# Attention and MLP on one core: the probabilities of ScalarE and VectorE in one array of 40 blocks, and a new order of the work

## The chip, the cores and the metric

The kernel runs on one core of a Trainium2 chip. The metric is the device time of one execution in microseconds; the time before is the median of three runs. Besides the times there is a profile of one execution: the instructions of each engine with start and duration, and for each idle stretch the work that ended it. Engines are TensorE (PE, with its weight loads as PEld), VectorE (DVE), ScalarE (ACT), GpSimd (POOL) and SyncE (SP), which only issues DMAs.

## The reference

A multi-head attention block and a mixer with an MLP run on the same input, and a gate mixes them for each token. S = 2048 tokens, D = 512, 32 heads of 16, F = 1792; inputs and output are bf16.

```python
g = sigmoid((x * gate_w).sum(-1, keepdims=True))
a = attention(x, wqkv, wo)                      # softmax over all 2048 keys, 32 heads
h = gelu(layernorm(x) @ w1)                     # its four quarters are shifted by 1, -1, 2, -2 tokens: hs
x1 = x + hs @ w2
b = x1 + gelu(layernorm(x1) @ w3) @ w4
return g * a + (1 - g) * b
```

Nearly all of the time goes to the softmax: 32 x 2048 x 2048 = 134 million exponentials.

## The kernel before

**Tiles and rounds.** The attention is cut into 32 rounds. A round is a chunk of 512 queries, a group of 8 heads and the even or odd heads of that group, so four heads run at once, one in each quarter of TensorE's rows. In a round each of the four heads has 16 key tiles of 128 keys; that makes 64 score tiles of 128 keys x 512 queries in a round and 2048 in all. A score tile is one matmul (line 1293) with 32 rows of weights; four of them, one for each quarter, can run side by side. Its result fills one of the eight PSUM banks.

**Two ways to the exponential.** ScalarE takes two or three score tiles (two or three banks) in one ACTIVATE with Exp and writes bf16 probabilities into two or three blocks of `pa_all`, an array of 16 blocks of 512 (`issue_act`, line 1376; the instruction is line 1388). VectorE takes single tiles and computes the bits of the bf16 result directly: one multiply and add from PSUM to 16-bit integers (line 1418). That gives a piecewise linear exponential, so three more copies of it are made, with 32, 64 and 96 added to the bits (`close_pair`, line 1433); the weighted sum of the four is close to the exponential. Two tiles of VectorE make a pair, and the copies are made for the pair, 1024 wide. The first copy is always VectorE's (line 1456). Of the second and third, GpSimd makes the third, or both, or none (line 1458 is GpSimd's): `GP2` is the share of pairs for which it makes both, `1 - GP3` the share, besides the pairs near the end of a round (`URG`), that VectorE makes alone. The pair and its copies lie in four of 12 buffers `PD` of 1024 each. At most three pairs are under way, which the class `token` counts.

**Products.** A tile of ScalarE costs one product with V (line 1510, `take_pv`), a tile of VectorE four, one for each copy, the last two with V scaled by 0.707. Products and all projections run in column mode, four side by side, one in each quarter of the columns; the scores run in row mode. Products sum up in one accumulator bank for each round. Lines 975 (`gen`) are the projections of attention and MLP, which are put between the attention's work and evacuated mostly by VectorE. At the end of a round the sums are copied out (line 1530), the denominators go through DRAM to be spread, and GpSimd multiplies (line 1546).

**The order.** No engine chooses anything on the chip: the order of every engine's instructions is fixed at build time by a planner in the kernel, the class `Sim` (line 152), which plays the engines through in time with a hold and a latency for each job. An exponential holds ScalarE for `0.833 * 512 * w + 67` ns, the first step of VectorE's tile `533 * w + 65` ns, a copy of a pair 338 ns on VectorE or 1018 ns on GpSimd. Copies on VectorE and all GpSimd jobs are marked `port`: the planner lets only one of them run at a time (`lock`, line 293). In the program itself each GpSimd job waits for the VectorE copy that stands before it in that order (`in_port_order`, line 267).

`pe_pick` (line 1678) chooses what TensorE does next. First come score tiles for ScalarE: twice in a row it tries to prepare three or two tiles, if the banks held for exponentials stay within `CAP3` or `CAP2`. With them, or when VectorE runs dry (`DVE_ALONE`), come score tiles for VectorE, as long as fewer than `DVE_WAIT` wait and fewer than `LIMD` other banks are taken (`room`). Then it fills the time until the running exponential ends with projections and products; products come first when many are ready (`PRESS`) or when few blocks of `PA` or buffers of `PD` are free (`PA_LOW`, `PD_LOW`). Every 8 score tiles the constants of these rules are changed by the table `STEPS` (line 453), which has 233 entries with 1482 values. So the number of tiles that VectorE gets, the size of each visit of TensorE to the scores, and the order of all queues follow from this table and from the holds.

**Buffers.** `Run` (line 49) takes several slots of a class at once. Banks must lie side by side. Two blocks of `PA` are simply the two lowest free ones; three must be evenly spaced.

```python
        pr = evs["pair"] = {"h": 0, "buf": Buf("PD", 8), "token": Buf("token", 1), "jobs": [], "pv": []}
```

A `PD` buffer is free again when the last of its copies and products has read it, for both tiles of the pair. The products of a pair, also those of the unshifted tiles, are queued only when the pair is closed, and wait for the first steps of both tiles.

Of the kernel before, what the change touches and what calls it, by code (L numbers as in the profile page):

```python
# [11 lines left out]
ALU = mybir.AluOpType  # L12
BF16 = mybir.dt.bfloat16
# [84 lines left out]
class Job:  # L98
    __slots__ = ("eng", "hold", "lat", "deps", "prio", "fn", "acq", "frees", "at", "done", "start", "seq", "ready", "name", "port", "watch", "deps_tiles")

    def __init__(self, eng, hold, lat, deps, fn, prio=5, acq=(), frees=(), at=0, name="", port=False):
# [7 lines left out]
        self.watch = []  # L109

# [41 lines left out]
class Sim:  # L152
# [4 lines left out]
    def __init__(self, slots):  # L157
# [13 lines left out]
        self.lock = 0.0  # L171
        self.pending = 0
# [109 lines left out]
    def try_engine(self, e):  # L282
# [27 lines left out]
        if j.port:  # L310
            self.lock = self.t + j.hold
        self.busy[e] += j.hold
# [3 lines left out]
        self.push(self.t + j.hold + j.lat, lambda: self.finish_job(j))  # L316
# [60 lines left out]
def kernel(  # L377
# [63 lines left out]
        PD_LOW=1,  # L441
        PA_LOW=0,
# [7 lines left out]
        ROT=2, DUE_SH=-14, AT_SH=0, HOLE=7, MAXG=1, CAP2=4, CAP3=0, LIMD=3, RES=0, ACC2=0, LIMA=3, JOIN=0,  # L450
# [3 lines left out]
        0: dict(DVE_STOP=8, SL0=165, AHEAD2=16, PV_IDLE=0.117, MAXU=4, LIMD=4, LIMA=2),  # L454
        1: dict(DVE_STOP=6, DVE_WAIT=1, AHEAD=16, PV_IDLE=0.5, MAXU=3, AT_SH=69, LIMD=3, LIMA=3),
        2: dict(P1_PRIO=0.743, GP2=0.5, DVE_STOP_L=16, DVE_WAIT=3, AHEAD=3, PV_IDLE=0.731, PRESS=15, DUE_SH=16, CAP2=6,
            RES=1, JOIN=1),
        3: dict(P1_PRIO=0.414, S_PRIO=0.3, DVE_STOP=13, DVE_STOP_L=14, EARLY=64, AHEAD=9, AHEAD2=24, PV_FULL=0.947,
            PRESS=18, CAP2=5, CAP3=6, RES=0),
        5: dict(S_PRIO=0.38, DVE_STOP=8, DVE_ALONE=-158, EARLY=99, AHEAD=3, PV_FULL=0.813, MAXU=9, ROT=1, AT_SH=96,  # L460
            HOLE=2),
        6: dict(MAXU=2),
        7: dict(GP2=0.315, URG_L=18, DVE_ALONE=2, AHEAD=9, PRESS=26, MAXU=3, CAP3=5),
        8: dict(URG_L=12, AHEAD=12, PV_FULL=0.916, PRESS=18, MAXU=4, AT_SH=69, HOLE=7, ACC2=1),
        9: dict(P1_PRIO=0.743, S_PRIO=0.625, EARLY=64, AHEAD=9, AHEAD2=13, PV_FULL=0.947, PV_IDLE=0.117, MAXU=5, ROT=3,
            HOLE=2, CAP3=6),
        10: dict(AHEAD=12, AHEAD2=24, LIMD=2),
        11: dict(URG_L=18),
        12: dict(P1_PRIO=0.279, GP2=0.655, URG_L=12, EARLY=99, AHEAD=9, AHEAD2=13, PV_FULL=0.916, MAXU=3, ROT=0, HOLE=3,
            LIMD=3, ACC2=0),  # L470
        13: dict(P1_PRIO=0.55, GP2=0.315, EARLY=64, IDLE_NS=700, DVE_WAIT=4, AHEAD2=5, MAXU=4, HOLE=7, MAXG=2),
        14: dict(P1_PRIO=0.743, URG_L=18, IDLE_NS=537, DVE_WAIT=3, AHEAD=12, AHEAD2=24, PV_FULL=0.947, MAXU=5, ROT=3,
            HOLE=2, MAXG=1, LIMD=2, ACC2=1),
        15: dict(DVE_WAIT=2),
        16: dict(URG_L=12, DVE_WAIT=3, AHEAD=9, HOLE=0, LIMD=3),
        17: dict(P1_PRIO=0.279, GP3=1, HOLE=2, MAXG=2),
        18: dict(P1_PRIO=0.743, GP3=0.967, EARLY=99, SL0=45, IDLE_NS=374, PD_LOW=3, AHEAD2=5, PV_FULL=0.916, HOLE=7,
            MAXG=1, CAP3=0, ACC2=0),
        19: dict(DVE_ALONE=-158, EARLY=64, SL1=0, IDLE_NS=459, AHEAD2=24, PV_IDLE=0.5, ROT=0),
        20: dict(URG=8, URG_L=18, SL1=60, IDLE_NS=374, PD_LOW=1, PV_FULL=0.97, PV_IDLE=0.117, HOLE=2),  # L480
        21: dict(URG=5, URG_L=12, SL1=0, IDLE_NS=459, PD_LOW=3, PV_FULL=0.916, PV_IDLE=0.5, HOLE=7),
        22: dict(HOLE=3),
        23: dict(DVE_STOP_L=12, HOLE=7),
        25: dict(DVE_STOP_L=14, URG=8, DVE_ALONE=2, IDLE_NS=864, PD_LOW=1, PA_LOW=3, AHEAD2=13, ROT=3, AT_SH=96, CAP2=6,
            LIMD=4, JOIN=0),
        26: dict(DVE_STOP=4, URG=5, URG_L=18, SL1=60, IDLE_NS=700, PD_LOW=3, PA_LOW=0, DVE_WAIT=4, AHEAD2=24,
            PV_IDLE=0.117, AT_SH=69, CAP2=5, LIMD=3, JOIN=1),
        27: dict(GP3=1, DVE_STOP=8, URG=8, EARLY=99, SL0=100, SL1=0, PD_LOW=2, DVE_WAIT=3, AHEAD=7, PV_FULL=0.947,
            PV_IDLE=0.5, HOLE=2, LIMA=2),
        28: dict(URG_L=12, SL0=45, IDLE_NS=374, AHEAD=9, DUE_SH=-6, HOLE=7, LIMA=3),  # L490
        29: dict(P1_PRIO=0.136, GP3=0.967, EARLY=64, IDLE_NS=864, AHEAD2=13, PV_FULL=0.916, PV_IDLE=0.731, DUE_SH=16,
            AT_SH=96, CAP2=6, LIMD=4, JOIN=0),
        30: dict(P1_PRIO=0.743, S_PRIO=0.178, GP2=1, DVE_STOP_L=16, URG=11, IDLE_NS=374, AHEAD2=24, PV_IDLE=0.5, ROT=0,
            AT_SH=69, CAP2=4, ACC2=1, JOIN=1),
        31: dict(S_PRIO=0.625, DVE_STOP_L=14, EARLY=99, PV_IDLE=0.731, ROT=3, CAP2=5, ACC2=0, JOIN=0),
        32: dict(DVE_STOP_L=16, EARLY=64, IDLE_NS=459, PA_LOW=1, PV_FULL=0.947, PV_IDLE=0.5, ROT=0, LIMA=4),
        33: dict(S_PRIO=0.178, DVE_STOP_L=7, URG=3, IDLE_NS=374, PA_LOW=0, AHEAD=12, PV_FULL=0.916, PRESS=11, ROT=2,
            AT_SH=118, ACC2=1, LIMA=3, JOIN=1),
        34: dict(S_PRIO=0.625, DVE_STOP_L=14, URG=11, IDLE_NS=864, PD_LOW=3, AHEAD=9, AHEAD2=9, PV_IDLE=0.117, PRESS=18,
            ROT=0, AT_SH=69, ACC2=0, JOIN=0),  # L500
        35: dict(SL1=60),
        36: dict(P1_PRIO=0.414, SL1=0, ACC2=1),
        37: dict(P1_PRIO=0.743, ACC2=0),
        38: dict(DVE_STOP_L=16, DVE_ALONE=-158, IDLE_NS=459, PD_LOW=2, PA_LOW=1, AHEAD2=24, PV_FULL=0.947, PRESS=57,
            MAXU=3, CAP3=5, LIMA=4),
        39: dict(P1_PRIO=0.55, S_PRIO=0.214, DVE_STOP_L=14, URG=2, DVE_ALONE=2, SL0=0, PD_LOW=3, AHEAD=5, PV_FULL=0.916,
            PRESS=18, MAXU=2, CAP2=4, CAP3=0, ACC2=1, LIMA=2, JOIN=1),
        40: dict(P1_PRIO=0.743, S_PRIO=0.625, URG=11, DVE_ALONE=-81, SL0=45, PD_LOW=2, AHEAD=9, PV_IDLE=0.5, PRESS=11,
            MAXU=5, ROT=1, ACC2=0, LIMA=4, JOIN=0),
        41: dict(SL0=165),  # L510
        42: dict(S_PRIO=0.214, GP3=0.8, SL0=45, AHEAD=7, PV_IDLE=0.117, PRESS=43, MAXU=4),
        43: dict(DVE_STOP_L=7, HOLE=3, CAP3=6),
        44: dict(SL1=60),
        45: dict(S_PRIO=0.178, DVE_STOP=6, DVE_STOP_L=12, DVE_ALONE=2, SL0=0, SL1=0, IDLE_NS=864, PV_FULL=0.947,
            PRESS=26, HOLE=2, CAP3=0, JOIN=1),
        46: dict(IDLE_NS=537, MAXG=2),
        49: dict(IDLE_NS=459, DUE_SH=32, MAXG=1),
        50: dict(JOIN=0),
        51: dict(S_PRIO=0.3, IDLE_NS=537, JOIN=1),
        52: dict(S_PRIO=0.178, IDLE_NS=459, MAXU=5, DUE_SH=16),  # L520
        53: dict(IDLE_NS=864, MAXU=4),
        54: dict(IDLE_NS=459, DUE_SH=32, LIMA=2),
        55: dict(PD_LOW=3, LIMA=4),
        56: dict(DVE_ALONE=138, PD_LOW=2, PA_LOW=0, JOIN=0),
        57: dict(DVE_STOP=4, DVE_STOP_L=14, URG=8, DVE_ALONE=362, EARLY=99, PD_LOW=3, PA_LOW=1, PV_FULL=0.97, DUE_SH=16,
            MAXG=2, ACC2=1),
        59: dict(DVE_STOP=6, DVE_STOP_L=12, URG=11, DVE_ALONE=2, EARLY=64, PD_LOW=2, PV_FULL=0.947, MAXU=5, MAXG=1,
            ACC2=0, JOIN=1),
        60: dict(DVE_STOP=4, DVE_STOP_L=14, URG=8, DVE_ALONE=362, EARLY=99, PD_LOW=3, PV_FULL=0.97, MAXU=4, ROT=2,
# [1389 lines left out]
```

## Time and profile before

| | |
|---|---|
| median of 3 runs (lowest to highest) | 762.45 us (760.06 to 764.45) |
| the profiled execution, its own time | 761.38 us |
| its span, first to last instruction | 759.4 us |
| TensorE clock granted, mean | 0.999 of full speed |
| ScalarE: first exponential starts, last one starts | 10.3 us, 749.5 us |
| ScalarE's busy time besides exponentials | five Gelu instructions (31.8 us) and table loads (12.8 us) |
| GpSimd's idle time before line 1458 | 255.0 us |
| all 16 DMA engines, mean | 46 GB/s; 17.40 MB read and 6.81 MB written in HBM |

A row of the costliest groups gives the line, the engine and the operation, what it writes and reads with shapes, how often it ran, then the busy time in us and the mean duration of one in ns, then the engine's idle time just before such instructions and whose work ended it. Instructions of one engine overlap at their ends, so busy time divided by count is less than the mean duration. A matmul's end is modelled: a TensorE that is 98% busy isn't at its peak. A row of the waits gives engine and line, who was waited for, the total in us, how often and the longest.

### The profile page before, as it was taken

What the parts mean: (1) busy time and instruction counts of PE and PEld (TensorE: products, weight loads), DVE (VectorE), ACT (ScalarE), POOL (GpSimd) and SP (SyncE); (2) the same over time, 40 slices, a digit from 0 to 9 for tenths busy, and PEclk for the clock granted to TensorE, in tenths of its full rate; (3) what the DMA queues carried; (4) which work ended last, traced back from release to release, by engine and by line L of the source; (5) the groups of instructions that cost most, each with busy time, mean ns of one, the idle gap of its engine ahead of it and who ended that gap; (6) DMA issues with size and microseconds to landing.
All of it is one profiled execution on the core that took longest, in us unless ns stands there. A gap on an engine that the chain in (4) does not pass through costs nothing.

```text
span 759.4 us, 23495 instructions
## 1 busy us (share of the span) xinstructions
PE 746.4 (98%) x9545; PEld 218.2 (29%) x9545; DVE 704.9 (93%) x1428; ACT 735.6 (97%) x744; POOL 460.4 (61%) x458
## 2 busy tenths in 40 slices
PE   9999999999999999999999999999999999999997
PEld 5343222222322222223222222422223222222332
DVE  6999899999999999999998999898999999999966
ACT  6999999999999999999998999999999999999995
POOL 2334476776785456775645767465466577767732
PEclk9999999999999999999999999999999999999999
DMA  9433211231001320042101000202000001000001
GB/s 189 150 87 58 53 47 33 48 100 65 21 6 48 79 68 13 15 133 65 38 15 33 27 20 21 47 11 58 23 27 19 15 17 28 26 27 21 20 16 34
DMA packets 67091, 34.57 MB, mean 46 GB/s; under 512 B 46748, under 2 KB 62380, under 8 KB 66984
## 3 DMA queue, kind: packets, MB, share of 16 engines
q1 hardware_dynamic: 66040, 32.56, 17.6%
q8 instruction: 74, 1.21, 0.7%
q10 hardware_dynamic: 944, 0.52, 0.2%
q14 instruction: 33, 0.27, 0.1%
HBM read 17.40 MB, written 6.81 MB: 32 GB/s over the span
## 4 chain that ended last, share of the span: by engine, by line
PE 72%; ACT 10%; DVE 9%; issue 3%; DMA 2%; POOL 2%; SPq 1%; POOLq 0%; DVEq 0%; ACTq 0%
PE banks L1510 25%; PE banks L1293 25%; PE banks L975 21%; ACT pa_all L1388 10%; DVE PD L1418 4%; DVE PD L1456 3%; POOL PD L1458 2%; DMA oD<-oT 1%; DMA pk<-den 1%; DMA xn_dram<-xn 1%; PE banks L954 0%; PE banks L1840 0%; SPq L1550 0%; POOL oT L1546 0%; PE banks L996 0%
## 5 line engine op out<-in xcount | busy, mean ns | idle before, releaser
L1388 ACT ACTIVATE pa_all<-banks 128x1024 bf16<-128x1024 f32 x719 | 685.7, 1137 | 9.8 <-PE banks L1293 7.9
L1458 POOL TENSOR_SCALAR PD<-PD 128x1024 uint16<-128x1024 uint16 x396 | 407.7, 1051 | 255.0 <-DVE PD L1456 117.8
L1418 DVE TENSOR_SCALAR PD<-banks 128x512 uint16<-128x512 f32 x554 | 366.3, 685 | 27.9 <-PE banks L1293 24.1
L1510 PE MATMUL banks<-PD,V 128*17 128x512 bf16 (+1 forms) x2240 | 300.2, 382 | 3.3 <-DVE PD L1456 1.5
L1293 PE MATMUL banks<-q,kT 32*128 32x512 bf16 x2048 | 288.8, 384 | 2.5 <-ACT pa_all L1388 1.3
L1510 PE MATMUL banks<-pa_all,V 128*17 128x512 bf16 (+1 forms) x1488 | 269.3, 381 | 0.0
L1456 DVE TENSOR_SCALAR PD<-PD 128x1024 uint16<-128x1024 uint16 x444 | 192.0, 476 | 1.4
L1293 PEld LDWEIGHTS <-kT 32*128 32x128 bf16 x2048 | 72.5, 91 | 313.9 <-ACT pa_all L1388 296.0
L1510 PEld LDWEIGHTS <-V 128*17 128x17 bf16 (+1 forms) x3728 | 72.5, 88 | 122.5 <-issue 104.3
L975 PE MATMUL banks<-xnT,w 128*32 128x512 bf16 x1152 | 95.6, 383 | 0.4 <-DVE PD L1418 0.2
L975 PE MATMUL banks<-w,hT 128*32 128x512 bf16 x704 | 59.6, 382 | 0.0
L975 PEld LDWEIGHTS <-w 128*32 128x32 bf16 x1920 | 43.6, 95 | 45.6 <-issue 27.4
L1546 POOL TENSOR_TENSOR oT<-accsb,bcs 128x512 bf16<-128x512 f32 x31 | 39.5, 1275 | 25.2 <-DVE PD L1456 16.0
L975 PE MATMUL banks<-w,hB 128*32 128x512 bf16 x448 | 43.0, 383 | 0.0
L975 PE MATMUL banks<-w,w 128*32 128x256 bf16 (+1 forms) x768 | 41.3, 311 | 0.0
L975 PE MATMUL banks<-wo,oD 128*32 128x512 bf16 x224 | 29.9, 383 | 1.2 <-DMA oD<-oT 1.1
L1530 DVE COPY accsb<-banks 128x512 f32<-128x512 f32 x31 | 21.1, 679 | 3.6 <-PE banks L1510 3.0
L975 PE MATMUL banks<-w,wq 128*32 128x512 bf16 x256 | 22.8, 383 | 0.3 <-ACT w L1006 0.3
L975 PEld LDWEIGHTS <-hT 128*32 128x32 bf16 x704 | 16.6, 95 | 18.9 <-issue 12.1
L1122 DVE BATCH_NORM_STATS2 st<-x_sb 128x6 f32<-128x512 bf16 x32 | 21.6, 683 | 0.1
L1212 DVE CAST hB<-banks 128x512 bf16<-128x512 f32 x28 | 18.9, 680 | 1.5 <-PE banks L975 1.4
L1212 DVE CAST hT<-banks 128x512 bf16<-128x512 f32 x28 | 18.8, 680 | 0.8 <-PE banks L975 0.7
(90 smaller groups left out, 253.9 us busy)
## 6 DMA issues: line engine op xcount, KB each, us to landing
bcs<-rr SPq DMA_DIRECT2D x124, 64.0 KB
xn_dram<-xn SPq DMA_DIRECT2D x32, 128.0 KB
w<-in_B_w_dram SPq DMA_DIRECT2D x5, 512.0 KB
oD<-oT SPq DMA_DIRECT2D x124, 16.0 KB
w<-in_B_w_dram SPq DMA_DIRECT2D x4, 448.0 KB
out_dram<-ot SPq DMA_DIRECT2D x14, 128.0 KB
x_sb<-in_A_x_dram SPq DMA_DIRECT2D x3, 512.0 KB
w<-in_A_wqkv_dram SPq DMA_DIRECT2D x2, 256.0 KB
```

The costliest lines, as they stand in the source:

```text
L975: units.append([Op("col", j, lambda j=j, lf=lf, rf=rf, n0=n0, n1=n1, st=st, sp=sp: nc.tensor.matmul(get()[32 * j:32 * j + 32, n0:n1], lhsT ...
L1122: a = dve(600, deps, lambda: nc.vector.bn_stats(out=sb.slot[:], in_=x_sb[:, t, :]), prio=6, at=at, acq=[sb])
L1212: pre.append(evac(g, PSUM_NS, lambda ps, m=m: nc.vector.tensor_copy(out=h2()[:, m, :], in_=ps[:])))
L1293: o = Op("row", i, lambda: nc.tensor.matmul(dst(), lhsT=kT[G][32 * i:32 * i + 32, kt * P:(kt + 1) * P], rhs=qbuf[G, c].slot[32 * i:32 * i ...
L1388: job = act(hold, ops, lambda: nc.scalar.activation(out=pa_all[:, pb.cut(), :], in_=unit()[:, rb.cut(), :], func=ACT.Exp, scale=0.25), acq ...
L1418: return nc.vector.tensor_scalar(out=pr["buf"].slot[:].rearrange("p (b c) -> p b c", c=512)[:, h0:h0 + w, :], in0=unit()[:, rb.cut(), :], ...
L1456: return nc.vector.tensor_scalar(out=d[k][:, 0:w], in0=d[0][:, 0:w], scalar1=float(SHIFT * k), scalar2=None, op0=ALU.add)
L1458: return nc.gpsimd.tensor_scalar(out=d[k][:, 0:w], in0=d[0 if both else 2][:, 0:w], scalar1=1.0, scalar2=float(SHIFT * (k if both else 1)) ...
L1510: return nc.tensor.matmul(one(accs[r])[32 * i:32 * i + n, :], lhsT=lhs(n), rhs=rhs(), start=st and not edge, stop=True, tile_position=(0, ...
L1530: e = dve(PSUM_NS, round_ops[r], lambda: nc.vector.tensor_copy(out=ab.slot[:], in_=one(accs[r])), acq=[ab], prio=0, frees=[accs[r], Call(a ...
L1546: n = gp(1250, d3, lambda: nc.gpsimd.tensor_tensor(out=ob.slot[:], in0=ab.slot[:], in1=bb.slot[:], op=ALU.mult), acq=[ob], frees=[ab, bb], ...
```

## The change

**One array.** `pa_all` (16 blocks) and the 12 `PD` buffers become `prob`, 40 blocks of 512 16-bit values; ScalarE writes into it as bf16, VectorE and GpSimd as integers. The number of tokens is 3 in both.

```diff
-    NPA, NPD, NW = 8, 12, 9
+    NPROB, NTOK, NW = 40, 3, 9
...
-    pa_all = const.tile([P, 2 * NPA, 512], BF16, name="pa_all")
+    prob = const.tile([P, NPROB, 512], U16, name="prob")
...
-        "PA": list(range(2 * NPA)),
-        "token": list(range((NPD - 1) // 3)),
-        "PD": slots("PD", NPD, [P, 1024], U16),
+        "PA": list(range(NPROB)),
+        "token": list(range(NTOK)),
+        "PD": [],
```

**Runs.** Two blocks are taken side by side from the shortest free stretch that holds them; where there is none, the two lowest free ones are taken, and the instruction then runs over two pieces. An exponential can be made to leave `spare` blocks free (`BRES`).

```diff
-    def __init__(self, cls, n):
-        self.cls, self.n = cls, n
-        self.bufs = [Buf(cls, 1) for _ in range(n)]
+    def __init__(self, cls, n, users=1, spare=0):
+        self.cls, self.n, self.spare = cls, n, spare
+        self.bufs = [Buf(cls, users) for _ in range(n)]
...
-        if len(free) < self.n:
+        if len(free) < self.n + self.spare:
             return None
         ids = sorted(free)
-        if self.cls == "bank":
+        if self.cls == "bank" or self.n == 2:
...
-            return None if best is None else [best[1] + h for h in range(self.n)]
+            if best is not None or self.cls == "bank":
+                return None if best is None else [best[1] + h for h in range(self.n)]
```

**Single release.** A pair and each of its copies is a run of two blocks; each block is freed when its own readers are done. The product of an unshifted tile is queued with its first step and waits for that step alone.

```diff
-            pr = evs["pair"] = {"h": 0, "buf": Buf("PD", 8), "token": Buf("token", 1), "jobs": [], "pv": []}
+            pr = evs["pair"] = {"h": 0, "buf": Run("PA", 2, 9), "token": Buf("token", 1), "jobs": [], "pv": []}
...
+        for h, (r, (kt, i)) in enumerate(tiles):
+            c, G, p = rounds[r]
+            add_pv(r, i, kt, lambda n, kt=kt, hd=8 * G + 2 * i + p: heads(V0, kt, hd, n),
+                   lambda b=b0.bufs[h0 + h]: prob[:, b.slot, :].bitcast(BF16), [j1, j_v[kt, G // 2]], b0.bufs[h0 + h])
...
-        bufs = [pr["buf"]] + [Buf("PD", pr["h"] + (k == 2)) for k in range(1, 4)]
-        pr["buf"].users = pr["h"] + (3 if both or alone else 2)
-        bufs[2].users = pr["h"] + (0 if both or alone else 1)
+        bufs = [pr["buf"]] + [Run("PA", pr["h"], 1 + (k == 2 and not (both or alone))) for k in range(1, 4)]
+        for b in pr["buf"].bufs[:pr["h"]]:
+            b.users += (4 if both or alone else 3) - 9
+        cut = lambda k: prob[:, bufs[k].cut() if pr["h"] == 2 else bufs[k].bufs[0].slot, :]
...
-                    return nc.vector.tensor_scalar(out=d[k][:, 0:w], in0=d[0][:, 0:w], scalar1=float(SHIFT * k),
-                                                   scalar2=None, op0=ALU.add)
+                    return nc.vector.tensor_scalar(out=cut(k), in0=cut(0), scalar1=float(SHIFT * k), scalar2=None,
+                                                   op0=ALU.add)
```

**The planner's rules.** A GpSimd job is planned only when the last VectorE job of the port has ended and its latency of 210 ns has passed as well. An exponential is planned with 55 ns beside its elements, not 67. Weight loads get a queue of their own speed. The weights of the MLP's second half are loaded at times 20 score tiles apart, not at once. Exponentials are prepared only while at most `GATE` banks are held for them. One limit, `B_LOW`, takes the place of `PD_LOW` and `PA_LOW`.

```diff
-            if j.port and self.lock > self.t or j.acq and any(not self.fits(b) for b in j.acq):
+            if j.port and (self.lock > self.t or e == "POOL" and self.dve_lock > self.t) or j.acq and any(not self.fits(b) for b in j.acq):
...
             self.lock = self.t + j.hold
+            if e == "DVE":
+                self.dve_lock = self.t + j.hold + j.lat
...
+        if e == "SP" and j.hold > 1.5:
+            if j.size:
+                self.queue = max(self.queue, self.t + j.hold) + j.size / 185.0
+            end = max(end, self.queue + 1500.0)
...
-        dl_w[name] = dma(6000.0, [], fn, acq=[wslot(name, users)], prio=2)
+        dl_w[name] = dma(4000.0, [], fn, acq=[wslot(name, users)], prio=2)
+        dl_w[name].size = 2 * src.shape[0] * src.shape[1]
...
-        hold = 0.833 * 512 * w + 67.0
+        hold = 0.833 * 512 * w + 55.0
...
-        dl_w[f"3{i}"].at = P_LD[0]
+        dl_w[f"3{i}"].at = P_LD[0] + 20 * i
...
-        dl_w[f"4{i}"].at = P_LD[1]
+        dl_w[f"4{i}"].at = P_LD[1] + 20 * i
...
-        for _ in range(2):
+        for _ in range(2 if act_banks[0] <= K.GATE else 0):
...
-        press = sum(cnt) > K.PRESS or len(sim.free["PA"]) <= 2 * K.PA_LOW + 1 or len(sim.free["PD"]) <= K.PD_LOW
+        press = sum(cnt) > K.PRESS or len(sim.free["PA"]) <= K.B_LOW
```

**The table.** `STEPS` is new as a whole: 214 entries with 477 values. Means over the 256 stretches of 8 tiles, worked out from both tables, before and after: `CAP2` 4.79 and 5.63 (6 in 13 and in 206 stretches), `CAP3` over 0 in 63 and 52 stretches, `GP2` 0.673 and 0.678, `GP3` 0.935 and 0.918, `DVE_WAIT` 2.82 and 3.05, `PRESS` 20.3 and 28.3, `MAXU` 5.2 and 3.3; `GATE` is 3 in 153 stretches, 4 in 51, 9 in 28 and 2 in 24.

More of the change, by code (lines that the diff above doesn't have):

```diff
@@ new lines @@
+        57: dict(B_LOW=2, AHEAD=3, ROT=0),
+        59: dict(GP2=0.5),
+        60: dict(AHEAD=12),
+        61: dict(JOIN=1),
+        63: dict(JOIN=0),
+        64: dict(P1_PRIO=0.279, GP2=0.315, GP3=1, IDLE_NS=537, B_LOW=5, BRES=4, AHEAD=24, PV_IDLE=0.731, PRESS=11,
+            MAXU=7, ROT=1, DUE_SH=-14, LIMD=4, GATE=3, ACC2=0, JOIN=1),
+        65: dict(S_PRIO=0.214, PV_IDLE=0.117),
+        66: dict(URG=8),
+        67: dict(CAP2=6),
+        68: dict(DVE_ALONE=-158, CAP3=5, LIMA=4),
+        69: dict(GP2=1, LIMA=2),
@@ L1377, in issue_act @@
         w = len(got)
-        rb, pb = Run("bank", w), Run("PA", w)
+        rb, pb = Run("bank", w), Run("PA", w, spare=int(K.BRES))
         sim.take(rb)
@@ L1469, in close_pair @@
         for h2, (r2, kt2, i2, G2, p2) in enumerate(pr["pv"]):
-            for k in range(4):
+            for k in range(1, 4):
                 hd = 8 * G2 + 2 * i2 + p2
```

536 lines of the change are left out of this document (229 added, 307 removed).

## The prediction

> **What bounds the kernel now.** I read the busy shares first, then the groups by shape, then one long stretch, then the waits, then the timeline. The busy shares show four engines and three of them nearly full.
>
> ```profile
> PE 746.4 (98%) x9545; PEld 218.2 (29%) x9545; DVE 704.9 (93%) x1428; ACT 735.6 (97%) x744; POOL 460.4 (61%) x458
> ...
> L1458 POOL TENSOR_SCALAR PD<-PD 128x1024 uint16<-128x1024 uint16 x396 | 407.7, 1051 | 255.0 <-DVE PD L1456 117.8
> L1418 DVE TENSOR_SCALAR PD<-banks 128x512 uint16<-128x512 f32 x554 | 366.3, 685 | 27.9 <-PE banks L1293 24.1
> ...
> L1456 DVE TENSOR_SCALAR PD<-PD 128x1024 uint16<-128x1024 uint16 x444 | 192.0, 476 | 1.4
> ```
>
> Line L1418 is VectorE's first step on a tile, L1456 and L1458 are the shifted copies of a pair. The groups by shape give ScalarE's exponentials and VectorE's few double first steps:
>
> ```profile
> L1388 ACT ACTIVATE pa_all<-banks 128x1024 bf16<-128x1024 f32 x669 | 628.5, 1106 | 9.7 <-PE banks L1293 7.9 <-PE banks L975 1.0 <-PE banks L1510 0.2
> ...
> L1388 ACT ACTIVATE pa_all<-banks 128x1536 bf16<-128x1536 f32 x50 | 77.2, 1543 | 0.1
> ...
> L1418 DVE TENSOR_SCALAR PD<-banks 128x1024 uint16<-128x1024 f32 x6 | 7.2, 1208 | 0.2 <-PE banks L1293 0.2
> ```
>
> So ScalarE has 2 x 669 + 3 x 50 = 1488 tiles and VectorE 548 + 2 x 6 = 560, together 2048. The sums of the stretch from 60 to 740 us, without head and tail (busy us of each engine, instructions in brackets):
>
> ```profile
> 60.00:740.00 680.00, 673.13 (x8373) 186.62 (x8374) 641.65 (x1282) 672.21 (x682) 435.84 (x422) 1.00 0.15 38
> ```
>
> ScalarE (fourth number) idles 680 - 672.2 = 7.8 us there, VectorE (third) 680 - 641.7 = 38.4 us. ScalarE is the bound. Time can only go if ScalarE gets fewer tiles, and that means that VectorE must take more of them. What a tile costs: the timeline of ScalarE shows 35 exponentials of two tiles in a row without a gap, so (32.46 - 1.106) / 34 = 0.922 us from start to start, **0.461 us a tile**.
>
> ```profile
> 298.79 32.46 ACT L1388 ACTIVATE pa_all<-banks 128x1024 bf16<-128x1024 f32 x35
> ```
>
> On VectorE a tile costs (366.3 + 192.0) / 560 = **0.997 us** of busy time. So every microsecond won for VectorE moves 1 / 0.997 tiles and takes 0.461 / 0.997 = 0.46 us off ScalarE, and off the end.
>
> Where VectorE loses time, the waits and the line's own durations (min/median/max) say:
>
> ```profile
> PEld L1293 <- ACT pa_all L1388: 296.0, 678, 2.1
> POOL PD L1458 <- DVE PD L1456: 117.8, 78, 9.0
> ...
> DVE PD L1418 <- PE banks L1293: 24.1, 65, 2.5
> ```
> ```profile
> L1456 DVE TENSOR_SCALAR PD<-PD x444: 355/416/1322, 12.7 to 749.0; 128x1024 uint16<-128x1024 uint16 x148
> ```
>
> VectorE waits 24.1 us for score tiles that TensorE has not yet made. And its shifts take 476 ns on average where the shortest takes 355: 444 x 0.121 = 53.7 us are lost inside them. The longest is 967 ns over the shortest, nearly one GpSimd shift (1051), so I read most of this as shifts that stand behind a GpSimd operation.
>
> The first row of the waits is TensorE: 678 times it comes to score matmuls and waits for an exponential to free its banks, once for nearly each of the 719 exponentials. The timeline shows what such a visit costs:
>
> ```profile
> 302.88 0.39 PE L1293 MATMUL banks<-q,kT 32*128 32x512 bf16 x3
> ...
> 303.20 0.39 PE L1510 MATMUL banks<-pa_all,V 128*17 128x512 bf16 x2
> 303.21 0.60 PE L1510 MATMUL banks<-PD,V 128*17 128x512 bf16 x5
> 303.43 0.38 PE L1510 MATMUL banks<-pa_all,V 128*17 128x512 bf16 x1
> ...
> 303.80 0.10 PEld L1293 LDWEIGHTS <-kT 32*128 32x128 bf16 x3 [0.49 <-ACT pa_all L1388]
> ```
>
> Four matmuls side by side take 0.22 us (303.20 to 303.43). From the scores to the next kind are 0.32 us, from the last of those to the next scores 0.37, so a visit costs 0.10 + 0.15 = 0.25 us beside its work. In a period of 0.92 us there is room for just two groups of four behind the scores: TensorE has little spare either.
>
> **The change part by part.**
>
> *One array of 40 blocks.* It is as large as before (16 blocks and 12 x 2). ScalarE waited 0.2 us for the reads of line L1510, and no VectorE shift waits for them by more than the 1.4 us of its row, so space as such binds neither; I take 0. GpSimd's waits behind L1510 are 25.9 us, off the path, since it idles 300 us. What the array can buy is freedom of order: probabilities may lie longer.
>
> *Single release, and the unshifted copy queued tile by tile.* No instruction more or less. A lone tile's first product no longer waits for its partner's first step (685 ns). TensorE has other products meanwhile; 0.
>
> *Pairs that lie apart.* Instructions over two blocks stay single ones. No row here shows a VectorE shift over two pieces. Lower end 0: line L1063 writes V in pieces of 16 at 677 ns, as the contiguous copies (680), but reads PSUM. Upper end: the rate of the double first step, 1208 - 476 = 0.73 us for each pair apart. The code takes adjacent blocks where it finds any, so I reckon one pair in ten apart (my choice): 0 to 44 x 0.73 = 32 us on VectorE. I take 0, since the nearest row by shape of the output shows no loss. On this the Trainium skill (VectorE: DVE Perf Modes, "What auto-detection actually checks") has a rule: a one-source operation keeps its fastest mode with 16-bit data, step 1 and an even outermost count, which two blocks apart satisfy. By it this term is 0, against the 32 of the upper bound; no run here shows it yet.
>
> *Scores in larger visits.* The limit of banks for exponentials (CAP2) is 6 in 206 of the 256 stretches of 8 tiles, where it was mostly 5 (177) or 4 (66); the new GATE, mostly 3, lets no exponential be prepared while more than three banks are held. So with two held, two exponentials are prepared in one visit, and the next end triggers none. If a third of the 678 visits goes: 226 x 0.25 = 56 us of TensorE time; ends 0 and, for half of them, 85. That is cover: it makes score tiles for VectorE come earlier. I credit a quarter of VectorE's idle time, 38.4 / 4 = **9.6 us**; ends -24 (the bank rival below) and +24.1, the whole wait.
>
> *GpSimd held until VectorE's port operation has landed* (dve_lock, 210 ns more in the plan only). The plan before let GpSimd start at once, while on the chip it waits for the semaphore, so shifts planned behind it met it late. I credit a quarter of the 53.7 us: **13.4 us**; ends 0 and 53.7.
>
> *The exponential planned at 853 + 55 = 908 ns* instead of 920; the trace says 922. Over some 690 exponentials the plan thinks ScalarE 690 x 14 = 9.7 us quicker than it is (before: 1.4). An ideal split would move 8.3 / (0.461 + 0.997) = 5.7 tiles, so the loss is 5.7 x 0.461 = **2.6 us**.
>
> *Shares that hardly move.* The mean of GP2 over the stretches goes from 0.673 to 0.678, of GP3 from 0.935 to 0.918: some 5 more shifts for VectorE among 280 pairs, 2 us; nothing. Three-wide exponentials are allowed in 52 stretches, not 63; a tile in one costs not over 1543 / 3 = 0.51 us, nothing either way.
>
> *DMAs.* Weight loads w3 and w4 start up to 60 tiles later each; TensorE waits 2.3 us in all for a DMA (L975 behind oD), so 0. Queue past which they move: SP's, which has room (DMA share 0.15).
>
> Sum: VectorE wins 9.6 + 13.4 = 23.0 us, which is 23 tiles; ScalarE loses 23 x 0.461 = 10.6 us. The 69 more products on TensorE (three more for each such tile) cost 69 / 4 x 0.22 = 3.8 us, covered by the visits saved, and if none are saved they eat the gain of the waits. The profiled execution took 761.4 us (span 759.4): 761.4 - 10.6 + 2.6 = 753.4; the median of the runs, 762.45, is 1.1 above it, so I say **754**.
>
> **The rivals.**
>
> *Banks run out (slower).* Six of eight banks for exponentials and one accumulator leave one for VectorE's tiles and all projections. For it: VectorE already waits 24.1 us for scores, nearly all of its waiting. Against: 43 stretches of the old order let triples have six banks too, and the longest of its waits was 2.5 us. If that wait doubles: 24.1 / 0.997 = 24 tiles go back to ScalarE, 11.1 us, and with the 2.6: **775**. It decides from where VectorE's busy share of 60 to 740 us falls below today's 94.4% by over 8 us (3.8 / 0.46), to 93.2%.
>
> *Port collisions stay (no change).* A shift meets GpSimd as often as GpSimd is busy, 407.7 of 759 us, and the change takes no work off GpSimd; then the 13.4 us stay lost: 762.4 - 4.4 + 2.6 = **760.6**. The skill states such a rule (SBUF — State Buffer, on the shared port pair): whichever of the two starts first holds the pair for its whole instruction. The longest shift, 967 ns over the shortest, agrees with it.
>
> *The array does not do what it says (no change).* Blocks of a pair are read in neighbouring groups and come free together, space never bound, and only the order is another one: **762**, give or take 4.
>
> *Pairs apart run slowly*: 32 us of VectorE unplanned, and 38.4 of idle time hide half: 16 us late, **778**.
>
> **How the numbers follow.** Forecast 0.48 (its own range 744 to 758, the upper from half the credit, the lower from twice it: 754 - 10); collisions stay 0.10 and only another order 0.10; banks 0.24; pairs apart or any other new wait 0.08. The collision case splits around the bound. A change of under 0.5%, 3.8 us, can't be told from none here. Faster by more: 0.50; within: 0.17; slower by more: 0.33. For 8 in 10 the range goes from 743 to 776: that leaves out the upper credits together and the case of pairs apart.
>
> **What would show it.** Right: about 583 tiles in L1418's successor, some 1465 in the exponentials, ScalarE's idle time still near 24 us, fewer than 500 waits of score matmuls for exponentials, shifts with a mean under 450 ns. Wrong: shifts whose shortest is no longer near 355 (mode lost), VectorE's wait for scores over 35 us (banks), ScalarE idle by over 15 us between 60 and 740, a mean of the shifts still at 476.

## The result, and the profile after

The changed kernel takes 811.28 us (median of 4 runs, 808.93 to 812.99), the kernel before in the same runs 762.87 us (760.06 to 764.45): 1.0637 times as long, with a 95% interval of 1.0595 to 1.0679. I had forecast 754, and 776 as the upper end of the range. It is slower, and not by a little.

The page of the changed kernel's profile gives the busy times, and ScalarE's busy tenths in 40 slices of the span:

```profile
span 807.1 us, 23686 instructions
...
PE 777.5 (96%) x9569; PEld 226.7 (28%) x9569; DVE 669.2 (83%) x1356; ACT 752.9 (93%) x754; POOL 427.0 (53%) x425
...
ACT  6999999999999998999985999999999099999996
```

ScalarE, the bound, is full in nearly all slices, but the 16th, 21st and 22nd show 8, 8 and 5, and the 32nd shows 0. The ledger of ScalarE splits the whole difference of the spans (807.1 - 759.4 = 47.7 us): it is busy for 752.9 us in place of 735.6, **17.3 us more**, and idles 807.1 - 752.9 = 54.2 us in place of 23.8, **30.4 us more**. The groups by shape tell where the first part is from, the exponentials now being line L1328 and VectorE's first steps L1359:

```profile
L1328 ACT ACTIVATE prob<-banks 128x1024 bf16<-128x1024 f32 x655 | 619.5, 1174 | 39.6 <-PE banks L1233 23.2 <-PE banks L1457 11.7 <-issue 3.2
L1328 ACT ACTIVATE prob<-banks 128x1536 bf16<-128x1536 f32 x74 | 115.3, 1581 | 0.4 <-PE banks L1233 0.3
```

That is 2 x 655 + 3 x 74 = 1532 tiles on ScalarE, and so 516 on VectorE; before they were 1488 and 560. VectorE did not win 23 tiles, it lost 44. At 0.461 us a tile that is 20.3 us, close to the 17.3. The waits of the same trace (engine and line, whom it waited for, us in total, times, longest) show what VectorE met:

```profile
PEld L1233 <- ACT prob L1328: 295.2, 639, 1.4
...
DVE prob L1359 <- PE banks L1233: 52.2, 106, 3.2
...
ACT prob L1328 <- PE banks L1233: 23.6, 7, 18.9
```

VectorE's wait for scores is up from 24.1 to 52.2 us, and TensorE still comes to the scores 639 times (678 before), not fewer than 500 times. The last row holds a single wait of ScalarE of 18.9 us, the 0 of the tenths. ScalarE's timeline around it (start and length of a run of instructions in us, how many, and in brackets the idle time ahead of it):

```profile
605.90 21.20 ACT L1328 ACTIVATE prob<-banks 128x1024 bf16<-128x1024 f32 x23
646.00 4.69 ACT L1328 ACTIVATE prob<-banks 128x1024 bf16<-128x1024 f32 x5 [18.90 <-PE banks L1233]
```

What TensorE does in this time stands in the chain that ends last, from 625 to 648 us:

```profile
625.35 0.37 PE banks L1233 x3
625.72 14.11 PE banks L915 x257
...
641.54 0.97 PE banks L1766 x24
642.52 2.16 PE banks L1457 x40
```

TensorE is not late with anything: it runs projections (L915) for 14 us, and then products (L1457) and fillers that add zeros (L1766), because the order that was written out for it holds no scores there. The other hole lies at 420 us, where ScalarE waits 9.18 us for products (line L1457) and some 4 us more in small pieces. Together the two holes are about 32 us, as much as the whole growth of ScalarE's idle time. In the smaller one TensorE does run dry, as its timeline shows (with VectorE's row that comes next):

```profile
424.21 0.09 PEld L915 LDWEIGHTS <-oD 128*32 128x32 bf16 x1 [3.46 <-DMA oD<-oT]
426.43 0.13 PEld L915 LDWEIGHTS <-oD 128*32 128x32 bf16 x2 [1.88 <-DMA oD<-oT]
427.93 0.75 DVE L1188 SCALAR_TENSOR_TENSOR ot<-banks,omg,x_sb 128x512 bf16<-128x512 f32 x1 [8.13 <-PE banks L915]
428.74 3.18 PE L1457 MATMUL banks<-prob,V 128*32 128x512 bf16 x28 [0.84 <-DVE ot L1188]
```

A projection of the attention's output (L915) stands in TensorE's order before its input `oD` has landed. VectorE waits for that projection, the products wait for VectorE, and ScalarE waits for a product to free a block: by the planner's books only one block is free at this place of the order, and an exponential needs two. How much of this hole belongs to the full array and how much to the transfer was not tested apart. SyncE issued these transfers only at 421.76 us; its queue held no weight load from 400 to 432 us.

### The profile page after: what moved, and what is told of

Read it like the earlier page. It is cut to its first block, busy times and chain, and to the rows that moved or that the text cites. A ratio compares the mean times of both kernels' runs of the same rounds, so it can differ in the third digit from the quotient of the medians.

```text
span 807.1 us, 23686 instructions
## 1 busy us (share of the span) xinstructions
PE 777.5 (96%) x9569; PEld 226.7 (28%) x9569; DVE 669.2 (83%) x1356; ACT 752.9 (93%) x754; POOL 427.0 (53%) x425
## 4 chain that ended last, share of the span: by engine, by line
PE 66%; ACT 22%; issue 4%; DVE 4%; DMA 2%; SPq 1%; POOL 0%; ACTq 0%; DVEq 0%; POOLq 0%
PE banks L1457 23%; PE banks L1233 23%; ACT prob L1328 20%; PE banks L915 18%; DVE prob L1359 1%; DVE prob L1402 1%; ACT hB L1153 1%; DMA xnT<-xn_dram 1%; PE banks L1766 1%; ACT L1328 1%; SPq L1490 0%; PE banks L894 0%; DMA oD<-oT 0%; PE banks L1787 0%; ACT hT L1153 0%
## 5 line engine op out<-in xcount | busy, mean ns | idle before, releaser
L1328 ACT ACTIVATE prob<-banks 128x1024 bf16<-128x1024 f32 (+1 forms) x729 | 703.0, 1215 | 40.0 <-PE banks L1233 23.6
L1404 POOL TENSOR_SCALAR prob<-prob 128x1024 uint16<-128x1024 uint16 x363 | 374.3, 1046 | 317.7 <-DVE prob L1402 137.9
L1359 DVE TENSOR_SCALAR prob<-banks 128x512 uint16<-128x512 f32 x515 | 342.9, 685 | 58.5 <-PE banks L1233 52.2
L1457 PE MATMUL banks<-prob,V 128*17 128x512 bf16 (+1 forms) x3596 | 331.8, 383 | 1.8 <-DVE ot L1188 0.8
L1233 PE MATMUL banks<-q,kT 32*128 32x512 bf16 x2048 | 288.9, 385 | 12.3 <-ACT prob L1328 10.2
L1402 DVE TENSOR_SCALAR prob<-prob 128x1024 uint16<-128x1024 uint16 x411 | 174.6, 463 | 15.4 <-PE banks L1457 10.1
L1233 PEld LDWEIGHTS <-kT 32*128 32x128 bf16 x2048 | 72.9, 91 | 330.7 <-ACT prob L1328 295.2
L1457 PEld LDWEIGHTS <-V 128*17 128x17 bf16 (+1 forms) x3596 | 75.5, 89 | 130.6 <-issue 106.8
L915 PE MATMUL banks<-xnT,w 128*32 128x512 bf16 x1152 | 95.4, 383 | 3.7 <-DMA xnT<-xn_dram 3.5
L915 PE MATMUL banks<-w,hT 128*32 128x512 bf16 x704 | 64.1, 383 | 0.0
L915 PEld LDWEIGHTS <-w 128*32 128x32 bf16 x1920 | 42.2, 95 | 50.4 <-issue 30.6
L915 PE MATMUL banks<-w,hB 128*32 128x512 bf16 x448 | 39.6, 382 | 0.0
L915 PE MATMUL banks<-w,w 128*32 128x256 bf16 (+1 forms) x768 | 38.9, 310 | 0.2 <-DVE prob L1359 0.2
L915 PE MATMUL banks<-wo,oD 128*32 128x512 bf16 x224 | 29.8, 385 | 4.4 <-DMA oD<-oT 4.4
L1188 DVE SCALAR_TENSOR_TENSOR ot<-banks,omg,x_sb 128x512 bf16<-128x512 f32 x12 | 9.0, 748 | 23.1 <-PE banks L915 23.1
L915 PE MATMUL banks<-w,wq 128*32 128x512 bf16 x256 | 24.0, 384 | 2.0 <-DVE prob L1359 1.3
L915 PEld LDWEIGHTS <-hT 128*32 128x32 bf16 x704 | 17.1, 95 | 19.5 <-issue 13.2
```

What stands on the lines that cost most here:

```text
L915: units.append([Op("col", j, lambda j=j, lf=lf, rf=rf, n0=n0, n1=n1, st=st, sp=sp: nc.tensor.matmul(get()[32 * j:32 * j + 32, n0:n1], lhsT ...
L1188: e = evac(g, PSUM_NS, lambda ps: nc.vector.scalar_tensor_tensor(out=ob.slot[:], in0=ps[:], scalar=omg[:, t:t + 1], in1=x_sb[:, t, :], op0 ...
L1233: o = Op("row", i, lambda: nc.tensor.matmul(dst(), lhsT=kT[G][32 * i:32 * i + 32, kt * P:(kt + 1) * P], rhs=qbuf[G, c].slot[32 * i:32 * i ...
L1328: job = act(hold, ops, lambda: nc.scalar.activation(out=prob[:, pb.cut(), :].bitcast(BF16), in_=unit()[:, rb.cut(), :], func=ACT.Exp, scal ...
L1359: return nc.vector.tensor_scalar(out=prob[:, b0.cut() if w == 2 else b0.bufs[h0].slot, :], in0=unit()[:, rb.cut() if w == 2 else rb.bufs[0 ...
L1402: return nc.vector.tensor_scalar(out=cut(k), in0=cut(0), scalar1=float(SHIFT * k), scalar2=None, op0=ALU.add)
```

## The experiments

Three theories stood against each other. **A**: the array costs nothing, the order does, since the table was not chosen well for the planner's new rules. **B**: the array itself costs time on the chip (two-piece instructions, releases across engines). **C**: one array for both kinds of probabilities lets the one crowd out the other. All kernels compute the same function; the place of the probabilities, the order and the split of the tiles between ScalarE and VectorE differ. The order's end in the expectations is the time of the last job by the planner's own holds: it says for what an order was written, and is no time of the chip.

### The array alone, and pairs apart

The kernel before, its table and planner untouched, with both kinds of probabilities in one array: first with each pair side by side, then with the halves of every pair 12 blocks apart.

```diff
-        job = act(hold, ops, lambda: nc.scalar.activation(out=pa_all[:, pb.cut(), :], in_=unit()[:, rb.cut(), :],
+        job = act(hold, ops, lambda: nc.scalar.activation(out=prob[:, pb.cut(), :].bitcast(BF16), in_=unit()[:, rb.cut(), :],
...
+    blk = lambda b, h: 16 + 2 * b.slot + h
```

In the second kernel the last line is

```diff
+    blk = lambda b, h: 16 + b.slot + 12 * h
```

> The kernel before with its own table, rules and order, only its buffers are laid into one array of 40 blocks: ScalarE's 16 blocks first, then each of the 12 pair buffers as two neighbouring blocks. Every engine's order stays as it was. Theory A (the loss is in the order that the planner makes, the array costs nothing by itself): 763 us, within 0.5%. Theory B (one array costs by itself, by waits between engines that touch it): over 770, with GpSimd's and VectorE's waits longer.

> As the first, but the two blocks of every pair lie 12 blocks apart, so all 444 shifts of VectorE and all 396 of GpSimd run over two pieces. Theory A: as the first run, shortest shift still near 355 ns. Rival (a shift over two pieces leaves its fast rate): shortest shift near 1.1 us, 444 x 0.73 us = 324 us more on VectorE, the time over 1000 us. If pieces cost only GpSimd: its shifts over 1.1 us and the time up by some 10 us.

Measured: 761.94 us, ratio 1.001 (0.9994 to 1.0025), and 761.41 us, ratio 0.9993 (0.9981 to 1.0005). The durations of VectorE's shifts in the second, min/median/max in ns:

```profile
L1459 DVE TENSOR_SCALAR prob<-prob x444: 355/418/1312, 12.0 to 748.7; 128x1024 uint16<-128x1024 uint16 x148
```

Before they were 355/416/1322. All 444 shifts now run over two pieces, and the shortest is the same. GpSimd's 396 stay at a median of 1047 ns (1048 before). The array and the two pieces cost nothing. The Trainium skill (VectorE: DVE Perf Modes, "What auto-detection actually checks") says so for a one-source operation on 16-bit data with step 1 and an even outermost count; the trace agrees. B is out as far as the pieces go.

### One rule alone: the exponential's hold

The kernel before with only the planned duration of an exponential changed.

```diff
-        hold = 0.833 * 512 * w + 67.0
+        hold = 0.833 * 512 * w + 55.0
```

> The kernel before with one number of the planner changed: an exponential is planned at 853 + 55 ns, not 853 + 67, as in the changed kernel; two pools, old table. The order comes out anew from the old table. Theory A (a table fits only the planner that it was chosen with): the planner's own last job moves from 751 to 774 us, so the time is 785 to 797 (the planner's end plus the 8 to 21 us by which the spans of the two known kernels lie over it). Theory B (the array): 763 to 766, since no array is in it.

Measured: 788.31 us, ratio 1.034 (1.0314 to 1.0366). I had priced this edit at 2.6 us; under the old table it costs 27 (before ran at 761.55 beside it). ScalarE is busy 744.6 us (9.0 more) and idles 787.4 - 744.6 = 42.8 us (19.0 more). No buffer and no kind of instruction is another one. Only the order is, and with it the split: VectorE has 542 tiles in place of 560.

### Two pools under the new rules

The changed kernel with the array split again into classes of 16 blocks for ScalarE and 24 for pairs.

```diff
-        "PA": list(range(NPROB)),
+        "PA": list(range(16)),
...
-        "PD": [],
+        "PD": list(range(16, NPROB)),
...
-        rb, pb = Run("bank", w), Run("PA", w, spare=int(K.BRES))
+        rb, pb = Run("bank", w), Run("PA", w, spare=0)
...
-        press = sum(cnt) > K.PRESS or len(sim.free["PA"]) <= K.B_LOW
+        press = sum(cnt) > K.PRESS or 2 * len(sim.free["PA"]) <= K.B_LOW or len(sim.free["PD"]) <= K.B_LOW
```

> The changed kernel with its table and its planner, but the 40 blocks are two pools again: 16 for ScalarE, 24 for the pairs (taken and released singly, as in the change). Theory A: the holes that come from a full array go (ScalarE idle 18.9 us at 627 us, 13 us at 420), but the order is still not fitted; the planner's last job is at 780, so 789 to 802 us. Theory B (the array): back to 765 to 770.

Measured: 791.2 us, ratio 1.0378 (1.0351 to 1.0406), so 20 us of the 48 go and 28 stay. ScalarE's longest wait for products is 4.3 us now, up to 424 us, and the larger hole is gone; but VectorE has no more tiles than before the split (513). So splitting gives the smaller part of the loss back, and this run alone can't say whether the space or the order did it, as splitting also writes another order.

### The hole at 627 us

At the start of the hole, as the planner in the kernel keeps its books, all 40 blocks are held, mostly by probabilities of round 25, whose accumulator may not be opened yet (`LIMA`), while round 24 still needs blocks for the copies of a pair. Two small edits of the table try this: a fourth bank for accumulators and others, or eight blocks that exponentials must leave free, both for a few stretches of 8 tiles only.

```diff
-        202: dict(GP2=0.315, DVE_ALONE=-158),
+        202: dict(GP2=0.315, DVE_ALONE=-158, LIMA=4),
...
-        205: dict(MAXU=3, AT_SH=96),
+        205: dict(MAXU=3, AT_SH=96, LIMA=3),
```
```diff
-        200: dict(P1_PRIO=0.312, LIMA=2),
+        200: dict(P1_PRIO=0.312, LIMA=2, BRES=8),
...
-        205: dict(MAXU=3, AT_SH=96),
+        205: dict(MAXU=3, AT_SH=96, BRES=0),
```

> The changed kernel; only the limit LIMA, up to which the next round may open its accumulator bank, is 4 instead of 3 in the stretches 202 to 204 of the table. The order is the same up to the place where ScalarE idles for 18.9 us (627 us in the profile). Theory C (the array is full of the next round's probabilities there, whose products may not start since no accumulator is open, so no block comes free): the hole shrinks to some 3 us and the time falls by the same, 811 - 15 = 796 us. Rival (the hole comes from the projections that stand there in TensorE's order): the hole stays, 811 us.

> The changed kernel; only BRES, the blocks that an exponential must leave free, is 8 instead of 0 in the stretches 200 to 204 of the table. Theory C: with blocks left for the pair that the old round still needs, that round can end; the hole shrinks to some 3 us, 793 to 797 us. Rival (the projections): the hole stays, 811 us.

Measured: 795.57 us, ratio 1.0423 (1.0394 to 1.0453), and 794.11 us, ratio 1.0415 (1.0377 to 1.0452): 15.7 and 17.2 us off the changed kernel. ScalarE's timeline at the place, with eight blocks left free:

```profile
609.59 18.50 ACT L1328 ACTIVATE prob<-banks 128x1024 bf16<-128x1024 f32 x20
630.90 29.49 ACT L1328 ACTIVATE prob<-banks 128x1024 bf16<-128x1024 f32 x32 [2.80 <-DVE prob L1402]
```

The wait of 18.90 us is now 2.80 (2.82 with the fourth bank). Either edit closes the hole, so C is shown for this one hole: about 16 us. The smaller hole lies ahead of the edited stretches and stays in both (a wait of 9.25 us with the fourth bank, 8.70 us with eight blocks left free). The larger one is a mishap at one place of one order and not what the array must cost, as the next run shows.

### The table chosen anew

The changed kernel, with array, runs, releases and rules as they are. 78 values of the table are changed in 38 of its stretches, one set after another, each kept if the order ended earlier. Its first lines:

```diff
-        0: dict(DVE_STOP_L=16, AHEAD2=16, MAXU=2, AT_SH=34, CAP3=6, GATE=9),
-        1: dict(CAP3=5),
+        0: {'DVE_STOP_L': 16, 'AHEAD2': 16, 'MAXU': 2, 'AT_SH': 34, 'CAP3': 6, 'GATE': 9, 'DVE_STOP': 8},
+        1: {'CAP3': 5, 'AHEAD2': 13},
...
-        5: dict(GP2=0),
+        5: {'GP2': 0, 'ROT': 1},
```

The two pools of the run above got the same treatment.

> The changed kernel with nothing changed but the table that steers its order: about 50 values of the 220 steps are chosen anew, one after another, so that the last job of the written-out order moves from 785.4 to 758.4 us. The array, the runs of blocks, the pairs that may lie apart, the single releases, the holds and the gate stay as they are; 516 tiles on VectorE, as before the refit. Theory A (the array and its rules cost next to nothing, the order on record was not fitted to them): the span lies 8 to 14 us over the order's end, as in the kernel before (8.5) and in the two pools under the new rules (9), so 767 to 773, and the two holes of ScalarE at 420 and 627 us are gone. Theory B (on the chip the shared array makes engines wait for each other's releases beyond what the order plans): the span lies 22 to 27 us over the order's end, as in the three one-array kernels so far, so 780 to 786. Theory C (one array for both kinds of probabilities runs full whatever the order): 795 or more.

> The two pools of the earlier run (16 blocks for ScalarE, 24 for pairs, all other new rules) with the table chosen anew in the same way: the order's end moves from 780.3 to 767.4 us, 519 tiles on VectorE. If what the chip adds to an order is about 9 us wherever the pools are separate, the span is 776 to 778 and the time 778 to 780; if it was only that order, up to 790. Beside the refitted one-array kernel: Theory A says that the one array is the faster by about the 9 us that its order ends earlier; Theory B says that it is slower by 2 to 8 us, since the shared releases cost it 13 to 18 us more than the separate ones.

Measured: the one array 774.34 us, ratio 1.0162 (1.0144 to 1.018); the two pools 788.52 us, ratio 1.0353 (1.0334 to 1.0371). The refitted array's page and timeline:

```profile
span 773.3 us, 23476 instructions
...
PE 754.1 (98%) x9470; PEld 218.8 (28%) x9470; DVE 669.5 (87%) x1398; ACT 752.5 (97%) x751; POOL 382.0 (49%) x380
...
ACT  6999999999999999999999999999999999999995
```
```profile
601.28 109.19 ACT L1330 ACTIVATE prob<-banks 128x1024 bf16<-128x1024 f32 x119
```

Other values in the table alone bring 37 of the 48 us back. The holes are gone; at the place of the larger one ScalarE now runs 119 exponentials in a row. Its busy time is 752.5 us as in the changed kernel (752.9), and its idle time 773.3 - 752.5 = 20.8 us in place of 54.2, less than the 23.8 of the kernel before. So the whole idle part of the loss was the order.

The span lies 14.9 us over the end that the order was written for, the two pools' 786.1 - 767.4 = 18.7 over theirs. So the 22 to 27 of theory B was wrong for the array, and B falls here too: the two pools lie further over their end than the array. A's 767 to 773 for the span was missed by 0.3 us, and its 8 to 14 over the end by 0.9. The two pools' span of 786.1 lies above the 776 to 778 that were expected if the chip always adds about 9 us to separate pools, so it does not. C falls: the array is not full whatever the order. That the array is 14 us faster than the two pools does not prove it the better: 9.0 of them lie in the orders' ends, and one search may have been luckier than the other. What remains between 759.4 and 773.3 is busy time of ScalarE: 16.9 us more, less 3.0 of idle time. VectorE still has only 516 tiles.

### GpSimd's lock, alone and taken out

First the kernel before with this one rule of the change; then the refitted array without it, its table chosen anew once more.

```diff
-            if j.port and self.lock > self.t or j.acq and any(not self.fits(b) for b in j.acq):
+            if j.port and (self.lock > self.t or e == 'POOL' and getattr(self,'dl',0.0) > self.t) or j.acq and any(not self.fits(b) for b in j.acq):
...
-                self.dve_lock = self.t + j.hold + j.lat
+                self.dve_lock = 0.0
```

> The kernel before with one rule of the change alone: GpSimd's jobs of the port are planned only when VectorE's last port job has landed. Table and pools stay, so the order is not fitted to the rule; it ends at 777.7 us in place of 750.9 and has 526 tiles on VectorE in place of 560. My prediction's term (the rule keeps shifts and GpSimd apart): the mean of VectorE's shifts falls from 476 ns to below 455. Theory A (any rule under a table that was not chosen for it costs more than it wins): time 787 to 800, ScalarE's busy time up by about 34 x 0.46 = 16 us, whatever the shifts do. Rival (the rule wins on the chip what the order can't show): below 775.

> The refitted one-array kernel with that one rule taken out and the table chosen anew for it in the same way: the order ends at 762.7 us, 515 tiles on VectorE, in place of 758.4 and 516. If the rule keeps shifts and GpSimd apart on the chip, the mean of VectorE's shifts rises from 441 ns to 465 or more, some 10 us of VectorE. If VectorE's share does not bind (it idles some 100 us there), the time goes by ScalarE's idle time alone: 762.7 + 8 to 19 = 771 to 782 for the span, whatever the shifts do.

Measured: the lock alone 790.21 us, ratio 1.0373 (1.0343 to 1.0403), within the 787 to 800 of theory A; the refit without the lock 781.53 us, ratio 1.0251 (1.022 to 1.0282), its span of 780.5 within the 771 to 782. The shifts of six kernels, from the groups by shape: the lock alone, the refit without it, the refit with it, the changed kernel, the hold alone (no lock) and the refitted two pools (with the lock); busy us, then mean ns:

```profile
L1458 DVE TENSOR_SCALAR PD<-PD 128x1024 uint16<-128x1024 uint16 x414 | 176.4, 466 | 2.7
```
```profile
L1407 DVE TENSOR_SCALAR prob<-prob 128x1024 uint16<-128x1024 uint16 x457 | 189.0, 452 | 8.5 <-PE banks L1462 3.3 <-ACT prob L1333 1.9 <-POOL prob L1409 0.3
```
```profile
L1404 DVE TENSOR_SCALAR prob<-prob 128x1024 uint16<-128x1024 uint16 x456 | 183.9, 441 | 9.8 <-PE banks L1459 6.2 <-POOL prob L1406 0.7 <-ACT prob L1330 0.2
```
```profile
L1402 DVE TENSOR_SCALAR prob<-prob 128x1024 uint16<-128x1024 uint16 x411 | 174.6, 463 | 15.4 <-PE banks L1457 10.1 <-issue 1.0 <-ACT prob L1328 0.7
```
```profile
L1456 DVE TENSOR_SCALAR PD<-PD 128x1024 uint16<-128x1024 uint16 x431 | 191.3, 486 | 4.3 <-PE banks L1510 2.2
```
```profile
L1399 DVE TENSOR_SCALAR prob<-prob 128x1024 uint16<-128x1024 uint16 x410 | 166.6, 446 | 12.1 <-PE banks L1454 9.3 <-POOL prob L1401 0.3
```

Put beside GpSimd's busy share, the means without the lock read 476 ns at 61% (before), 486 at 57% and 452 at 48%; with it 466 at 56%, 446 at 55%, 463 at 53% and 441 at 49%. The share alone does not order them. At like shares the kernel with the lock has the shorter shifts, by 452 - 441 = 11 ns in the refits and by 486 - 466 = 20 ns between the hold alone and the lock alone. That is 456 x 0.011 = 5.0 to 414 x 0.020 = 8.3 us of VectorE; the refitted two pools would make it more, and as every pair also differs in its order, the size isn't settled. Both expectations missed: not below 455 ns with the lock alone (466), and not 465 or more without it in the refit (452). The longest shift of the refit with the lock is still 1317 ns, 958 over its shortest: VectorE still stands behind whole GpSimd instructions. The refit without the lock was written to end 762.7 - 758.4 = 4.3 us later and is 7.2 us slower; which part of this the lock made, and which the other order, can't be told. And alone under the old table the lock moves 34 tiles to ScalarE, which is busy 750.6 us there, 15.0 more than before (I had reckoned 16), and idles 787.6 - 750.6 = 37.0 us.

## Why the prediction was wrong, step by step

**The step that failed.** It is the one that stands unspoken under every term of the sum: that the new table drives the new planner about as well as the old table drove the old one, so that each rule could be priced by itself and the prices added. I read the table through means of its values (`CAP2`, `GP2`, `GP3`, `MAXU`) and put most of them under "shares that hardly move". The runs show that one rule under a table not chosen for it costs 27 us (the hold) or 29 us (the lock: 790.21 - 760.75), whatever the rule is worth, and that other values alone give 37 of the changed kernel's 48 us back.

- *One array, "space as such binds neither; I take 0".* Right for the array under the old order: +0.1%, not told from none. Wrong for the order that came: there the blocks run out at 627 us, and about 16 us hang on it. I looked at who waits for space in the trace of before; but an order that leaves probabilities lying longer makes its own shortage, and the planner answers it with stretches that hold no scores, so the trace shows a wait for TensorE (L1233) and none for a block.
- *DMAs, 0.* Wrong for the order that came, though not by the weight loads that the term was about: TensorE's 3.46 and 1.88 us of waiting for `oD` lie in the smaller hole, some 13 us of ScalarE's idle time; how much of it hangs on them was not tested. I had gone by the 2.3 us of such waits in the trace of before.
- *Pairs apart, 0 of 0 to 32 us.* Right, by 444 shifts apart.
- *Larger visits, +9.6 us for VectorE.* Wrong in sign: its wait for scores is 52.2 us, not 14.5, and the visits are 639, not under 500. In its signs the rival *banks run out* came true (a wait over 35 us; VectorE busy less than 93.2% of 60 to 740 us), and it gave 775. But its mechanism isn't shown: with the hold alone or the lock alone VectorE waits for scores about as long, and there the old `CAP2` and no `GATE` hold.
- *The lock, +13.4 us for VectorE.* The kernels with the lock have the shorter shifts, but by some 5 to 8 us of VectorE, not 13.4, as far as the pairs tell; and VectorE has idle time in which that is lost.
- *The hold, 2.6 us.* It cost ten times as much under the old table (27 us), since I priced an ideal split and not the order that follows.
- *0.46 us off the end for each microsecond of VectorE.* The price of a tile held: 44 tiles by 0.461 are 20.3 us, and ScalarE's busy time rose by 17.3. The rest is a slightly cheaper tile, 703.0 / 1532 = 0.459 us (line L1328) in place of 685.7 / 1488 = 0.461 (L1388).
- *Only another order: 762, give or take 4.* This rival named the cause, but 4 us was far too small a scatter: nine orders under new rules or values ran from 774 to 811 us, all of them slower.

The waits for scores in the lock's run, for the point on banks:

```profile
L1420 DVE TENSOR_SCALAR PD<-banks 128x512 uint16<-128x512 f32 x522 | 346.9, 682 | 64.6 <-PE banks L1295 57.4 <-POOL PD L1460 2.3 <-POOL oT L1548 1.1
```

**What stays open.** Every order under the new rules gives VectorE 513 to about 521 tiles, 526 with the lock alone, 542 with the hold alone and 560 before. Without the lock the refit has 515, so the lock isn't the only reason. That tiles lie on ScalarE costs the refitted kernel its last 17 us; whether some table would give VectorE 560 under these rules, and then beat the kernel before, was not found out. Nor do the runs explain why the span exceeds the order's end by 8 to 9 us under the order of before (8.5 in the kernel before) and by 9 to 27 us under the others. No version here beats the kernel before; the array with the old order equals it.

## What to carry to other kernels

Where the order of the work is written out by a planner with hand-picked or searched constants, a changed rule is two changes: the rule, and an order that nobody chose. Price the second first, by the scatter of orders under small changes of the constants, and don't add up gains of rules that are smaller than that scatter. To learn what a new layout of buffers is worth, run it first under the old order, where it can only cost, and then with the constants chosen anew, where it can gain.

A shared pool needs a rule that keeps enough free for the work that sets blocks free again; two pools keep some free by their split. When it failed here, the profile named the engine that should have brought the work (TensorE), not the pool: look at what the supposedly late engine was doing in the gap. In the larger hole it was busy with other work, in the smaller one it waited itself.

## What the runs showed of the hardware that I had not expected

A VectorE shift and a GpSimd shift over two pieces 12 blocks apart take the same time as over one (355 against 355 ns at the shortest, 1047 against 1048 at the median). And the granted clock of TensorE was 0.83 in the stretch of the smaller hole, where TensorE was busy only 14.78 of 20 us (busy us of PE, PEld, VectorE, ScalarE and GpSimd, then the clock), while it was 1.00 in the larger hole, which TensorE fills:

```profile
420.00:440.00 20.00, 14.78 (x171) 4.43 (x164) 7.17 (x14) 6.68 (x8) 7.42 (x7) 0.83 0.13 38
627.00:646.00 19.00, 19.00 (x346) 8.75 (x339) 7.04 (x11) 0.11 (x1) 1.75 (x2) 1.00 0.09 30
```

Right behind TensorE's wait for `oD` in the smaller hole, 28 products took 3.18 us, or 0.45 us for four, where the prediction's stretch shows 0.22: by these numbers some 1.6 us (an estimate) on top of the gap itself. No run here separates this part.
